# Attention bias of the first head pair in a buffer of its own, one reciprocal write per pair, and token chunks of 512 first queries

## Chip, cores and metric

One Trainium2 chip, one core. The metric is the device time of one execution in microseconds (us). The kernel before took 1145.42 us (median of three runs, 1142.89 to 1146.14).

## What is computed

Attention with a relative-position bias (batch 8, 8 heads, 576 positions, head size 64), and then a gated two-layer network on its 4608 tokens. The sizes below are those of the inputs; everything is float32.

```python
def _attn_ref(q, k, v, w1, b1, w2):
    B, H, S, D = q.shape                        # 8, 8, 576, 64
    scores = (1.0 / np.sqrt(D)) * np.matmul(q, k.transpose(0, 1, 3, 2))
    pos = np.arange(S)
    rel = (pos[:, None] - pos[None, :]).astype(np.float32)
    psi_rel = np.log1p(np.abs(rel))
    psi_i = np.log1p(np.maximum(pos[:, None].astype(np.float32), 1.0))
    x = (psi_rel / psi_i)[..., None]
    h = np.maximum(x @ w1 + b1, 0.0)            # hidden 32
    bias = h @ w2                               # one value per (i, j, head)
    scores = scores + bias.transpose(2, 0, 1)[None, :, :, :]
    scores = scores - np.max(scores, axis=-1, keepdims=True)
    attn = np.exp(scores)
    attn = attn / (np.sum(attn, axis=-1, keepdims=True) + 1e-09)
    return np.matmul(attn, v).astype(np.float32)

def _moe_ref(x, w1, w2, w3, w_out):             # x: 4608 x 512
    a = x @ w1                                  # 512 x 1024
    b = x @ w2
    h = a * b @ w3                              # 1024 x 1024
    return (h @ w_out).astype(np.float32)       # 1024 x 512
```

## The kernel before

It has four stages on one core, and each engine's order within them comes from a table of times that is sorted (`ORDER`, `FIRST`, `AT_...`, one number per step). The table fixes PE (matmuls), ACT (ScalarE), DVE (VectorE) and POOL (GpSimd) up to what the tile scheduler lets float; the order on SP, the queue that issues nearly all DMAs, is the scheduler's own. An engine and a queue run strictly in order: what stands behind a waiting instruction waits too.

**Prologue: the bias.** The bias depends on i, j and the head alone, so it is made once for all batches. There are 36 groups `G` of 16 rows i. For each group DVE or ACT makes the hidden layer in four parts (`hidden`, L507 on DVE into `zdve`, 14 buffers; L505 on ACT into `zact`, 6 buffers), PE multiplies by w2 (L522, `bacc`, four PSUM buffers, one or two per group), ACT copies the result, 16 rows x 8 heads on the 128 partitions, to `bev` (L535), and SP writes it to the DRAM tensor `nb_d` (L537), one row of 591 values per row i and head. A `bev` has four buffers (`ep`), so the copies of a group wait for the write of the group four before. The wide groups come first: 576 columns in group 0, 304 around group 18, 576 again in group 35.

`load_bias` (L237 to L240) reads the bias back from `nb_d` as tiles of 128 rows of one head: tiles 0 to 7 (four blocks of 128 rows, even for the first head of the pair, odd for the second) and tile M, the last 64 rows of both heads. A block needs groups up to 7, 15, 23 or 31; M needs all 36.

**Attention.** 32 units, one for each pair of heads `p` and batch `b`. For each unit SP loads q, k and v (`rq`, `rk`, `rv`; those of the first unit's q and k go through ACT's queue), POOL splits q and k into a high and a low part for exact products (`op_g`, L266 and L267: `kh`, `kl`, `qh`, `ql`), PE makes the scores of nine tiles (`op_S`, L283, two PSUM buffers `s`), DVE adds the bias and takes the maximum (`op_T`, L294, needs `nb`), ACT the exponential (`op_E`, L319), PE transposes (L340 and others), and multiplies by v (`op_W`, L403). On DVE the tiles of a unit run in the order 3, 2, 5, 6, 1, 0, M, 4, 7. The output `x` of a unit is not yet divided by the sums and goes to the DRAM tensor `x_d[p]` with one write (L416). At the end of a pair the 72 sums of its eight batches are inverted, transposed to `rt` (L363), and written to `r_d[p]` with two writes per batch, sixteen in all (L329, L330).

**Folding.** Since nothing nonlinear stands between w3 and w_out, the kernel multiplies them once (`fold`, L608 to L628, `wacc` on PE), beside the last units. At the same time the up-projection weights come in as 64-bit numbers and are narrowed (`narrow`: load `wi` at L129, L134 and L138 on ACT, L144 to L166 on DVE, L171 and L172 on POOL, `wi` has two buffers), then split into `wh` and `wl`. ACT and DVE interleave this with the high and low parts of w3 (`w3h` L619, `w3l` L621) and with the split of the first x chunk.

**Chunks.** The 4608 tokens go through the network in nine chunks of 512, in their order in memory. For each, SP loads x and the reciprocals of four pairs (`load_x`: `xr` L643, `rb` L646, a row of r_d broadcast to 64 partitions), DVE multiplies and splits (`split_x`, L652, L658, with POOL's L656 between), PE does the up (L670) and down (L695) products, and SP writes 4 x 128 rows out (L706). The last chunk's output is split over ACT and DVE (L710 to L713).

Of the kernel before, what the change touches and what calls it, by code (L numbers as in the profile page):

```python
# [65 lines left out]
def relpos_attention_moe(  # L66
# [161 lines left out]
    def load_bias(p, t, first=False):  # L228
# [92 lines left out]
    def op_r(u, n):  # L321
        p, b = units[u]
        if n == "":
            nc.vector.tensor_scalar(sums[p], sums[p], 1e-9, None, op0=ALU.add)
            nc.vector.reciprocal(sums[p], sums[p])
        else:
            for c in range(B):
                rows, x = r_d[p][:, c * S:(c + 1) * S], rts[p][9 * c:9 * c + 9]
                nc.sync.dma_start(rows[:, 0:512].rearrange("h (i j) -> h i j", j=P), x[0:8])  # L329
                nc.sync.dma_start(rows[:, 512:S].rearrange("(o h) j -> o h j", o=1), x[8:9])  # L330
# [83 lines left out]
    def op_x(u, n):  # L414
        p, b = units[u]
        nc.sync.dma_start(x_d[p][:, b * S:(b + 1) * S], st[u]["x"])  # L416
# [32 lines left out]
    with ExitStack() as pro:  # L449
        sb = pro.enter_context(tc.tile_pool(name="pro", bufs=1))  # L450
        zp = pro.enter_context(tc.tile_pool(name="zp", bufs=14))
        ep = pro.enter_context(tc.tile_pool(name="ep", bufs=4))
# [59 lines left out]
        def bias_group(G):  # L512
# [16 lines left out]
            for c, acc in zip((0, 512), accs):  # L529
# [6 lines left out]
            r0 = G * GR * NB_W + 1  # L536
            nc.sync.dma_start(  # L537
                nb_d[:, r0:r0 + GR * (NB_W + 1)].rearrange("h (i w) -> i h w", i=GR)[:, :, 0:L + R + 1], ev,
            )
# [31 lines left out]
    NT = CH // P  # L571
    STEP = 7.8
# [67 lines left out]
    def load_x(c):  # L640
        for cc in range(NC):
            xr = xs.tile([P, CH], F32, name=f"xr{cc}", bufs=1)
            nc.sync.dma_start(xr, x_d[cc][:, c * CH:(c + 1) * CH])  # L643
            rb = xs.tile([P, CH], F32, name=f"rb{cc}", bufs=1)
            for h, rows in enumerate((lo, hi)):
                nc.sync.dma_start(rb[rows], r_d[cc][h:h + 1, c * CH:(c + 1) * CH].broadcast_to([64, CH]))  # L646
# [40 lines left out]
    def down(c, ft):  # L687
# [140 lines left out]
```

## Time and profile before

| | us |
|---|---|
| median of the runs | 1145.42 |
| the profiled execution | 1145.79 |
| its span, first to last instruction | 1144.0 |
| PE busy | 1103.3 |
| DVE busy | 632.2 |
| ACT busy | 564.4 |
| POOL busy | 372.0 |
| granted PE clock, mean | 0.989 |

The page divides the span into 40 slices and gives each engine's busy tenths in each; its fourth part is the chain of work that ended last, its fifth the costliest groups of instructions with the idle time before them and what ended it. Rows of busy time by stretches read: start and end, length, busy time of PE, PE's weight loads, DVE, ACT and POOL with their numbers of instructions, then the granted PE clock, the busy share of the 16 DMA engines, and GB/s. A timeline row has the start, the duration, the engine, the line, the operation, output <- input, shapes, the count of merged instructions, and in brackets the idle time before it with what ended it. SPq and ACTq rows are DMA issues: their time is that of the issue, not of the transfer.

### The profile page before, as it was taken

The page shows a single profiled execution, that of the slowest core. Times are in us where ns is not written, and L with a number is a line of the kernel's source. Part 1 is how long each engine was busy: PE and PEld are TensorE (multiplying, and loading weights), DVE is VectorE, ACT ScalarE, POOL GpSimd, SP SyncE. Part 2 cuts the span into 40 slices and gives each one's busy share as a digit, 9 for nine tenths or more (in the row PEclk, how much of TensorE's full clock was granted, in tenths as well). Part 3 has the DMA queues.
Part 4 walks back from the last instruction along what each step waited for, and adds up shares of the span by engine and source line. Part 5 has one row for each costly group of instructions (what it writes and reads, how often), then busy time and mean ns, then how long its engine had stood idle before and what let it go on. Part 6 is the DMA issues. An engine that isn't in the chain of part 4 may idle for free.

```text
span 1144.0 us, 22667 instructions
## 1 busy us (share of the span) xinstructions
PE 1103.3 (96%) x9092; PEld 865.1 (76%) x9092; DVE 632.2 (55%) x1267; ACT 564.4 (49%) x1119; POOL 372.0 (33%) x286
## 2 busy tenths in 40 slices
PE   7669999999999999997999999999999999999998
PEld 3147777777777777775888888888888888888886
DVE  8748997998799799878992312222131312223112
ACT  6669988998898899853542121121212112121211
POOL 0346775676677577364450000000000000000000
PEclk9889999999999999998999999999999999999999
DMA  7874575557555644226331202021121102110101
GB/s 210 259 216 122 176 223 169 158 153 238 155 177 187 190 148 150 89 83 178 111 129 38 74 9 83 19 74 38 53 59 37 56 19 74 37 37 1 37 1 37
DMA packets 61513, 123.15 MB, mean 108 GB/s; under 512 B 9696, under 2 KB 19296, under 8 KB 61408
## 3 DMA queue, kind: packets, MB, share of 16 engines
q1 hardware_dynamic: 60112, 120.21, 33.7%
q8 instruction: 71, 1.16, 0.4%
q10 hardware_dynamic: 1296, 1.49, 0.4%
q14 instruction: 34, 0.28, 0.1%
HBM read 91.76 MB, written 29.92 MB: 106 GB/s over the span
## 4 chain that ended last, share of the span: by engine, by line
PE 82%; DMA 3%; ACT 2%; DVE 2%; issue 1%; POOL 1%; SPq 1%; ACTq 0%; DVEq 0%; POOLq 0%
PE up L670 32%; PE o L695 16%; PE pst L403 14%; PE s L283 13%; PE pst L340 6%; DMA wi<-in_moe_w_dram 2%; PE wacc L628 1%; POOL w L171 1%; ACT pt L365 1%; DMA rb<-r_d 1%; PE pst L347 1%; PE pst L351 0%; ACT pp L319 0%; SPq L329 0%; DVE w3l L621 0%
## 5 line engine op out<-in xcount | busy, mean ns | idle before, releaser
L294 DVE CUSTOM_DVE_ANT_0 ts<-s,nb 128x576 f32<-128x576 f32 x288 | 210.6, 754 | 56.5 <-PE s L283 31.7
L678 DVE TENSOR_TENSOR g<-up,a 128x512 f32<-128x512 f32 x72 | 49.7, 690 | 332.3 <-PE up L670 332.3
L670 PE MATMUL up<-xl,wh 128*128 128x512 f32 x576 | 225.0, 391 | 0.0
L670 PE MATMUL up<-xh,wl 128*128 128x512 f32 x576 | 224.9, 391 | 0.0
L670 PE MATMUL up<-xh,wh 128*128 128x512 f32 x576 | 224.9, 391 | 0.0
L319 ACT ACTIVATE pp<-ts,mx 128x576 f32<-128x576 f32 x256 | 195.8, 771 | 20.7 <-DVE mx L294 18.9
L695 PE MATMUL o<-w3s,gh 128*128 128x512 f32 x576 | 177.4, 389 | 0.0
L403 PE MATMUL pst<-pt,rv 128*64 128x256 f32 (+1 forms) x1280 | 167.5, 407 | 0.6 <-DVE rt L363 0.4
L656 POOL TENSOR_SCALAR xh<-xr 128x512 fp32r<-128x512 f32 x36 | 24.4, 677 | 441.6 <-DVE xr L652 438.2
L675 ACT COPY a<-up 128x512 f32<-128x512 f32 x72 | 42.2, 585 | 247.3 <-PE up L670 247.3
L365 ACT ACTIVATE pt<-pst 128x1024 f32<-128x1024 f32 x128 | 124.1, 1019 | 23.4 <-PE pst L340 23.4
L403 PEld LDWEIGHTS pst<-pt,rv 128*64 128x64 f32 x1280 | 87.6, 136 | 62.2 <-issue 9.0
L681 ACT ACTIVATE gh<-g 128x512 fp32r<-128x512 f32 x72 | 45.5, 632 | 174.6 <-DVE g L678 174.6
L283 PE MATMUL s<-kh,qh 64*128 64x288 f32 x640 | 118.6, 366 | 10.9 <-DVE mx L294 8.7
L670 PEld LDWEIGHTS up<-xh,wl 128*128 128x128 f32 x576 | 108.1, 188 | 23.5
L670 PEld LDWEIGHTS up<-xl,wh 128*128 128x128 f32 x576 | 108.1, 188 | 23.3
L670 PEld LDWEIGHTS up<-xh,wh 128*128 128x128 f32 x576 | 108.1, 188 | 23.3
L695 PEld LDWEIGHTS o<-w3s,gh 128*128 128x128 f32 x576 | 108.1, 188 | 22.7
L695 PE MATMUL o<-w3s,gl 128*128 128x512 f32 x288 | 112.3, 390 | 0.5 <-DVE gl L684 0.5
L340 PE MATMUL pst<-ident,pp 64*128 64x64 f32 x2304 | 102.1, 223 | 0.7 <-ACT pt L365 0.7
L340 PEld LDWEIGHTS pst<-ident,pp 64*128 64x128 f32 x2304 | 96.9, 139 | 6.5 <-ACT pt L365 5.7
L283 PE MATMUL s<-kh,ql 64*128 64x288 f32 x640 | 96.1, 294 | 2.4 <-POOL ql L267 2.4
(92 smaller groups left out, 1655.1 us busy)
## 6 DMA issues: line engine op xcount, KB each, us to landing
rq<-in_q_dram SPq DMA_DIRECT2D x31, 640.0 KB
wi<-in_moe_w_dram SPq DMA_DIRECT2D x32, 512.0 KB
nb_d<-bev SPq DMA_DIRECT2D x36, 295.5 KB
rv<-in_v_dram SPq DMA_DIRECT2D x32, 320.0 KB
x_d<-x SPq DMA_DIRECT2D x32, 288.0 KB
xr<-x_d SPq DMA_DIRECT2D x36, 256.0 KB
rb<-r_d SPq DMA_DIRECT2D x72, 128.0 KB
rk<-in_k_dram SPq DMA_DIRECT2D x31, 288.0 KB
```

The costliest lines, as they stand in the source:

```text
L283: nc.tensor.matmul(s[:, hf, :HS], Q[x][rows, q0:q0 + P], K[y][rows, h * HS:(h + 1) * HS], start=(m == 0), stop=(m == len(ops) - 1),)
L294: nc.vector.tensor_tensor_reduce(out=halves(ts), in0=d.pop(("s", t))[:, :, :HS], in1=halves(NB[p, t]), op0=ALU.add, op1=ALU.min, scale=-1. ...
L319: nc.scalar.activation(pp, ts, AF.Exp, bias=mx, scale=-1.0, accum_out=sums[p][:, 9 * b + col:9 * b + col + 1])
L340: nc.tensor.transpose(ps[0:n, hf, c0:c0 + 64], x[rows], ident[rows, rows])
L365: nc.scalar.activation(o, x, AF.Copy)
L403: nc.tensor.matmul(o, x[:, c0:c0 + D], m, start=(c == 0), stop=(c == 4 and n_m == len(ms) - 1),)
L656: nc.gpsimd.tensor_scalar(xh, xr, 1.0, 1.0, op0=ALU.mult, op1=ALU.mult)
L670: nc.tensor.matmul(acc, l[:, cc], r, start=(n == 0), stop=(n == 3 * NC - 1))
L675: nc.scalar.copy(a, ps[0])
L678: nc.vector.tensor_tensor(g, ps[1], a, op=ALU.mult)
L681: nc.scalar.activation(gh, g, AF.Copy)
L695: nc.tensor.matmul(d["o", t], l[:, sl], folded[ft][r], start=(ft == 0 and n == 0), stop=(ft == NF - 1 and n == 2),)
```

## The change

Five edits, which hang together.

1. The bias of heads 0 and 1 gets a DRAM tensor of its own, `nb_0`. The host reorders the columns of w2 so that the heads of pair 0 are every fourth partition of `bev`. Each group is now written twice: first the 32 partitions of pair 0 to `nb_0`, and, as a step of its own with its own pace (`PACE_D`), all 128 to `nb_d`. The first pair's tiles are read from `nb_0`. `bev` has 18 buffers.
2. The loads of the first unit's q and k and their splits come earlier in the table (`FIRST`).
3. `r_d[p]` takes the layout of `rt`, 8 batches x 9 rows x 128, so that one write of 72 rows replaces sixteen.
4. `x_d[p]` holds the first 512 queries of the eight batches and then their last 64 queries, in two writes per unit. A chunk is one batch's first 512 queries; the eight times 64 last queries form a chunk, which runs eighth, before batch 7 (`SEQ`). Loads and output rows follow; the outputs of that chunk are eight writes of 64 rows.
5. The pool `sm` is opened ahead of `ppool` and `pt`, so it lies at other addresses.

```diff
-LEAD, PACE_B, BUSY_D, BUSY_A, LAG_B = 48.00, 1.25, 1.95, 4.50, 6.15
-FIRST = {"ldk": -15.0, "ldq": -14.0, "ldv": -4.0, "gk": -9.0, "gq": -5.0}
+LEAD, PACE_B, PACE_D, BUSY_D, BUSY_A, LAG_B = 48.00, 1.25, 2.20, 1.95, 4.50, 6.15
+FIRST = {"ldk": -38.0, "ldq": -36.0, "ldv": -4.0, "gk": -32.0, "gq": -30.0}
...
-    r_d = [dram.tile([2, NTOK], F32, name=f"r_d{p}") for p in range(NPAIR)]
+    r_d = [dram.tile([B, 9, P], F32, name=f"r_d{p}") for p in range(NPAIR)]
...
-            rows = nb_v[2 * p + h, r0:r0 + o.shape[0], :]
+            rows = (nb_v[h * NPAIR + p] if p else nb_v0[h])[r0:r0 + o.shape[0], :]
...
-            for c in range(B):
-                rows, x = r_d[p][:, c * S:(c + 1) * S], rts[p][9 * c:9 * c + 9]
-                nc.sync.dma_start(rows[:, 0:512].rearrange("h (i j) -> h i j", j=P), x[0:8])
-                nc.sync.dma_start(rows[:, 512:S].rearrange("(o h) j -> o h j", o=1), x[8:9])
+            nc.sync.dma_start(r_d[p].rearrange("b n j -> (b n) j"), rts[p])
...
-        nc.sync.dma_start(x_d[p][:, b * S:(b + 1) * S], st[u]["x"])
+        nc.sync.dma_start(x_d[p][:, b * 512:(b + 1) * 512], st[u]["x"][:, 0:512])
+        nc.sync.dma_start(x_d[p][:, B * 512 + b * 64:B * 512 + (b + 1) * 64], st[u]["x"][:, 512:S])
...
-        ep = pro.enter_context(tc.tile_pool(name="ep", bufs=4))
+        ep = pro.enter_context(tc.tile_pool(name="ep", bufs=18))
...
-            r0 = G * GR * NB_W + 1
-            nc.sync.dma_start(
-                nb_d[:, r0:r0 + GR * (NB_W + 1)].rearrange("h (i w) -> i h w", i=GR)[:, :, 0:L + R + 1], ev,
-            )
+            for nb, x in ((nb_0, ev[0:P:NPAIR]), (nb_d, ev)):
+                r0 = G * GR * NB_W + 1
+                nc.sync.dma_start(nb[:, r0:r0 + GR * (NB_W + 1)].rearrange("h (i w) -> i h w", i=GR)[:, :, 0:L + R + 1], x)
+                yield
...
-            put(plan, bias_group(G), *(at + d for d in AT_BIAS))
+            put(plan, bias_group(G), *(at + d for d in AT_BIAS), min(-LEAD + AT_BIAS[-1] + 1.0 + G * PACE_D, -0.3 + 0.005 * G))
...
+    sm = att.enter_context(tc.tile_pool(name="sm", bufs=2))
     ppool = att.enter_context(tc.tile_pool(name="ppool", bufs=1))
     pt = att.enter_context(tc.tile_pool(name="pt", bufs=1))
-    sm = att.enter_context(tc.tile_pool(name="sm", bufs=2))
...
+    SEQ = [*range(B - 1), B, B - 1]
...
-            nc.sync.dma_start(xr, x_d[cc][:, c * CH:(c + 1) * CH])
+            nc.sync.dma_start(xr, x_d[cc][:, k * CH:(k + 1) * CH])
...
-                nc.sync.dma_start(rb[rows], r_d[cc][h:h + 1, c * CH:(c + 1) * CH].broadcast_to([64, CH]))
+                if k < B:
+                    o, r = rb[rows], r_d[cc][k:k + 1, 4 * h:4 * h + 4].rearrange("o i j -> o (i j)").broadcast_to([64, CH])
+                else:
+                    o = rb[rows].rearrange("p (b j) -> p b j", b=B)
+                    r = r_d[cc][:, 8, 64 * h:64 * h + 64].rearrange("b (o j) -> o b j", o=1).broadcast_to([64, B, 64])
+                nc.sync.dma_start(o, r)
...
+                if k == B:
+                    nc.scalar.copy(o, d["o", t])
+                    for e, part in enumerate((lo, hi)):
+                        r0 = (2 * t + e) * S + 512
+                        nc.sync.dma_start(out[r0:r0 + 64, :], o[part])
...
-    w2 = inputs["w2"]
+    w2 = inputs["w2"].reshape(hid, pairs, 2).transpose(0, 2, 1).reshape(hid, heads)
```

Three places show what moves. The first is PE's row in the prologue. Before, the first unit's scores (L283) come behind the bias groups 30 (496 columns) and 31 (512), in the midst of group 32:

```order
L522 MATMUL bacc<-zdve,w2b 32x496 x3
L522 MATMUL bacc<-zact,w2b 32x496
L522 MATMUL bacc<-zdve,w2b 32x512 x6
L283 MATMUL s<-kh,qh 128x288 x2
L283 MATMUL s<-kh,ql 128x288
L522 MATMUL bacc<-zact,w2b 32x512
```

In the changed kernel they (now L286) stand between groups 13 (368 columns) and 14 (352), on the way to the narrow ones:

```order
L523 MATMUL bacc<-zdve,w2b 32x368 x4
L286 MATMUL s<-kh,qh 128x288
L523 MATMUL bacc<-zdve,w2b 32x352 x3
L286 MATMUL s<-kh,qh 128x288
L286 MATMUL s<-kh,ql 128x288 x2
L523 MATMUL bacc<-zact,w2b 32x352
L523 MATMUL bacc<-zdve,w2b 32x336 x4
```

22 of the 36 groups now stand behind the first scores, where 4 did.

The second place is SP at the end of the bias, where the loads of tiles 6 and 7 (128x576, and 128x512 with 128x64) and of M (the rows with 64 partitions) are issued. Before:

```order
L237 DMA nb<-nb_d 128x576
L537 DMA nb_d<-bev 16x8x591 x2
L239 DMA nb<-nb_d 128x512
L240 DMA nb<-nb_d 128x64
L254 DMA rq<-in_q_dram 128x1280
L237 DMA nb<-nb_d 64x576
L239 DMA nb<-nb_d 64x512
L240 DMA nb<-nb_d 64x64
```

In the changed kernel (nb_98 is `nb_0`):

```order
L539 DMA nb_98<-bev 16x2x591
L240 DMA nb<-nb_98 128x576
L242 DMA nb<-nb_98 128x512
L243 DMA nb<-nb_98 128x64
L539 DMA nb_d<-bev 16x8x591 x16
L240 DMA nb<-nb_98 64x576
L242 DMA nb<-nb_98 64x512
L243 DMA nb<-nb_98 64x64
L257 DMA rq<-in_q_dram 128x1280
```

Sixteen whole writes now stand between the loads of tiles 6 and 7 and those of M.

The third is SP at the passage from attention to chunks. Before, the loads of the first chunk (xr and rb, four pairs) come ahead of the fifth and sixth weight load:

```order
L129 DMA wi<-in_moe_w_dram 128x4x256 x2
L643 DMA xr_9401<-x_d_98 128x512
L416 DMA x_d_101<-x 128x576
L646 DMA rb_9403<-r_d_102 64x512 x2
L643 DMA xr_9406<-x_d_99 128x512
L646 DMA rb_9408<-r_d_103 64x512 x2
L643 DMA xr_9411<-x_d_100 128x512
L646 DMA rb_9413<-r_d_104 64x512 x2
L643 DMA xr_9416<-x_d_101 128x512
L646 DMA rb_9418<-r_d_105 64x512 x2
L129 DMA wi<-in_moe_w_dram 128x4x256 x2
```

In the changed kernel:

```order
L416 DMA x_d_102<-x 128x512
L417 DMA x_d_102<-x 128x64
L129 DMA wi<-in_moe_w_dram 128x4x256
L647 DMA xr_9410<-x_d_99 128x512
L655 DMA rb_9412<-r_d_103 64x512 x2
L647 DMA xr_9415<-x_d_100 128x512
L655 DMA rb_9417<-r_d_104 64x512 x2
L647 DMA xr_9420<-x_d_101 128x512
L655 DMA rb_9422<-r_d_105 64x512 x2
L647 DMA xr_9425<-x_d_102 128x512
L655 DMA rb_9427<-r_d_106 64x512 x2
L129 DMA wi<-in_moe_w_dram 128x4x256
```

The fifth weight load moved ahead of the twelve loads of the first chunk, and the sixth stayed behind them.

More of the change, by code (lines that the diff above doesn't have):

```diff
@@ L199, in relpos_attention_moe @@
     nb_d = dram.tile([H, (S + 1) * NB_W], F32, name="nb_d")
-    nb_v = nb_d[:, 0:S * NB_W].rearrange("h (i w) -> h i w", w=NB_W)[:, :, NB_L:NB_L + S]
+    nb_0 = dram.tile([2, (S + 1) * NB_W], F32, name="nb_0")
+    nb_v, nb_v0 = (
+        x[:, 0:S * NB_W].rearrange("h (i w) -> h i w", w=NB_W)[:, :, NB_L:NB_L + S] for x in (nb_d, nb_0)
+    )
     x_d = [dram.tile([P, NTOK], F32, name=f"x_d{p}") for p in range(NPAIR)]
-    r_d = [dram.tile([2, NTOK], F32, name=f"r_d{p}") for p in range(NPAIR)]
+    r_d = [dram.tile([B, 9, P], F32, name=f"r_d{p}") for p in range(NPAIR)]
     att, att_r = ctx.enter_context(ExitStack()), ctx.enter_context(ExitStack())
@@ L571, in relpos_attention_moe @@
     NT = CH // P
+    SEQ = [*range(B - 1), B, B - 1]
+    assert NCH == B + 1 and S - 64 == CH
     STEP = 7.8
@@ L640, in load_x @@
     def load_x(c):
+        k = SEQ[c]
         for cc in range(NC):
             xr = xs.tile([P, CH], F32, name=f"xr{cc}", bufs=1)
-            nc.sync.dma_start(xr, x_d[cc][:, c * CH:(c + 1) * CH])
+            nc.sync.dma_start(xr, x_d[cc][:, k * CH:(k + 1) * CH])
             rb = xs.tile([P, CH], F32, name=f"rb{cc}", bufs=1)
             for h, rows in enumerate((lo, hi)):
-                nc.sync.dma_start(rb[rows], r_d[cc][h:h + 1, c * CH:(c + 1) * CH].broadcast_to([64, CH]))
+                if k < B:
[4 more added lines that the diff above has]
+                nc.sync.dma_start(o, r)
             chunks[c]["x"][cc] = (xr, rb)
@@ L702, in down @@
                 o = op.tile([P, DO], F32, name="osb")
-                rows = out[c * CH + t * P:c * CH + (t + 1) * P, :]
-                if c < NCH - 1:
+                k = SEQ[c]
+                r0 = min(k, B - 1) * S + t * P
+                rows = out[r0:r0 + P, :]
+                if k == B:
[3 more added lines that the diff above has]
+                        nc.sync.dma_start(out[r0:r0 + 64, :], o[part])
+                elif c < NCH - 1:
                     nc.scalar.copy(o, d["o", t])
```

## The prediction

> **What bounds the kernel now.** Three views in this order: the page for the share of each engine, the busy time by stretches to see where TensorE (PE) is not full, and the timelines of those stretches to see what ends each gap.
>
> ```profile
> span 1144.0 us, 22667 instructions
> PE 1103.3 (96%) x9092; PEld 865.1 (76%) x9092; DVE 632.2 (55%) x1267; ACT 564.4 (49%) x1119; POOL 372.0 (33%) x286
> ...
> 50.00:60.00 10.00, 5.05 (x21) 1.47 (x23) 1.09 (x3) 5.00 (x12) 9.17 (x6) 0.54 0.59 166
> ...
> 70.00:80.00 10.00, 4.21 (x62) 3.96 (x62) 2.80 (x8) 4.65 (x12) 1.26 (x1) 0.73 0.70 212
> ...
> 300.00:400.00 100.00, 99.57 (x1459) 78.30 (x1461) 85.69 (x197) 89.22 (x182) 68.08 (x50) 1.00 0.58 180
> ...
> 520.00:550.00 30.00, 23.93 (x89) 18.09 (x88) 24.98 (x33) 10.53 (x19) 14.97 (x12) 0.89 0.50 152
> 550.00:1144.00 594.00, 589.46 (x2587) 485.02 (x2585) 179.87 (x260) 121.32 (x209) 45.37 (x50) 1.00 0.15 48
> ```
>
> The second number of a window is its length, the third PE's busy time. PE is full in the attention (99.57 of 100 us) and in the chunks (589.46 of 594). So a change pays only where PE is not full: the bias prologue with the first unit (about 50 to 85 us) and the passage from attention to chunks (about 510 to 540). The profiled execution took 1145.79 us, 1.8 more than its span and 0.4 more than the median of the runs shown; I forecast from 1145.8.
>
> In the first place VectorE (DVE) tells what the first unit waits for:
>
> ```profile
> 5.95 45.14 DVE L507 TENSOR_SCALAR zdve<-tsh,beta 128x576 f32<-128x576 f32 x126
> ...
> 60.69 0.76 DVE L294 CUSTOM_DVE_ANT_0 ts<-s,nb 128x576 f32<-128x576 f32 x1 [9.61 <-PE s L283]
> ...
> 68.21 0.76 DVE L294 CUSTOM_DVE_ANT_0 ts<-s,nb 128x576 f32<-128x576 f32 x1 [4.18 <-DMA nb<-nb_d]
> ...
> 76.68 0.76 DVE L294 CUSTOM_DVE_ANT_0 ts<-s,nb 128x576 f32<-128x576 f32 x1 [6.10 <-DMA nb<-nb_d]
> ```
>
> DVE makes bias inputs without a gap until 51.1, waits 9.6 us for the first scores, and at last for the bias of tile M, the seventh of the unit, until 76.68. DVE works in order, so the unit's last two tiles and all later units stand behind it. **The gate of the prologue is the moment M's bias lands.**
>
> **The change, part by part. The bias.** 36 quarter writes come on top of the 36 whole ones. The queue rows in the section on the change put M's load behind the last 16 whole writes. So nearly all bias traffic still stands ahead of M. The rate and the sizes:
>
> ```profile
> q1 hardware_dynamic: 8066, 15.88, 76.9%
> ...
> nb_d<-bev SPq DMA_DIRECT2D x36, 295.5 KB
> nb<-nb_d SPq DMA_DIRECT2D x5, 288.0 KB
> ...
> 10.85 11.44 SPq L537 DMA_DIRECT2D nb_d<-bev  x10
> ...
> 72.31 0.60 SPq L240 DMA_DIRECT2D nb<-nb_d  x1
> ...
> 40.00:50.00 10.00, 6.57 (x44) 1.82 (x44) 10.00 (x26) 6.69 (x16) 4.19 (x1) 1.00 0.95 318
> ```
>
> The first row is of 10 to 77 us: 15.88 MB in 76.9% of 67 us is 308 GB/s while the engines are busy (318 GB/s at a share of 0.95 around 45 us). A whole write is 0.303 MB, a quarter 0.076, a tile of bias 0.295. From 10.85 us until M lands the changed queue moves 36 x 0.303 + 36 x 0.076 + 9 x 0.295 + two units' q and k (1.90) = 18.2 MB: 59 us at 308 GB/s, so M lands no earlier than 70, and about 74 with 2 us of slow start and 2 us from transfer to use. That would be 2.7 us better than 76.68.
>
> But the scores move too. PE's rows put the first of them (kh,qh) between bias groups 13 and 14, and they need GpSimd (POOL) to split q and k. What POOL does beside DVE's stream:
>
> ```profile
> 45.81 5.80 POOL L266 TENSOR_SCALAR kh<-rk 128x576 fp32r<-128x576 f32 x1 [44.50 <-DMA rk<-in_k_dram]
> ...
> L266 POOL TENSOR_SCALAR kh<-rk x32: 669/680/5804, 45.8 to 455.4; 128x576 fp32r<-128x576 f32 x32
> L266 POOL TENSOR_SCALAR qh<-rq x32: 1260/1268/1279, 53.1 to 451.1; 128x1280 fp32r<-128x1280 f32 x32
> ...
> L267 POOL TENSOR_TENSOR kl<-rk,kh x32: 1401/1427/1434, 51.7 to 456.1; 128x576 fp32r<-128x576 f32 x32
> L267 POOL TENSOR_TENSOR ql<-rq,qh x32: 2880/2932/2942, 54.4 to 452.5; 128x1280 fp32r<-128x1280 f32 x32
> ...
> 23.63 2.29 PE L522 MATMUL bacc<-zdve,w2b 128*32 128x368 f32 x12
> ...
> 17.54 1.78 ACT L535 ACTIVATE bev<-bacc,post 128x480 f32<-128x480 f32 x4
> ...
> 41.53 0.34 ACTq L254 DMA_DIRECT2D rk<-in_k_dram  x1
> ```
>
> The split that takes 0.68 us (median) took 5.80 beside the stream, and ended 0.5 us after the stream did: it stood still for as long as DVE ran. I read this as POOL being kept out by a DVE that never pauses. In the change k is asked for within the copies of 17.54, near 18 us, and lands near 22 (4.3 us passed from the request at 41.53 to 45.81), beside the same stream; PE reaches its first score behind the 368-wide group (23.63 here), at about 25.4. Then: PE waits; DVE runs on for its 14 buffers, at 45.14/126 = 0.36 us each or somewhat less (these are narrow), to about 29.5; it stops, and POOL does kh, kl, qh and ql in 0.7 + 1.4 + 1.3 + 2.9 = 6.3 us. Both streams go on at about 36, group 14 is copied out by 37.5, and the stream of inputs ends near 57 in place of 51.1.
>
> Queued behind the wait: bias groups 14 to 35 on PE, their copies on ACT, and on SP the next quarter write, with everything behind it. By then SP has sent 14 quarters, 8 whole writes, two tiles of bias and the first q and k, 5.0 MB or 16 us: the DMA engines run dry near 28 and stand until 37.5. What is left to M is 22 x 0.076 + 28 x 0.303 + 7 x 0.295 + 0.95 = 13.2 MB, 42.7 us: 80.2, and 2 more to use: **82, or 5.5 us later than 76.68.** All behind M moves with it: POOL has the second unit's q and k long before, and PE's two score buffers are full at M, now as before. At 252 GB/s, the mean of 15.88 + 0.95 MB over those 67 us, M would be at 92 and at 335 (318/0.95) at 79. I take 308, the rate of this very stretch.
>
> *The lock.* The Trainium skill, "SBUF — State Buffer", section "Who interferes with whom", says that a two-port DVE instruction and a GpSimd instruction exclude each other only for one whole instruction. By that, POOL would wait for one input of some 0.4 us and not for thirteen; the sum would be 74 and not 82. The 5.80 row speaks against it, though it is one case.
>
> **The reciprocals.** Sixteen writes per pair become one, 60 fewer in all. For the last pair SP spent 485.72 to 495.5 on them, and just behind stood what comes now:
>
> ```profile
> 485.72 0.60 SPq L329 DMA_DIRECT2D r_d<-rt  x1
> ...
> 495.56 0.35 SPq L416 DMA_DIRECT2D x_d<-x  x1
> ...
> 493.68 1.66 POOL L171 TENSOR_TENSOR w<-w,wi 128x512 f32<-128x512 f32 x1 [2.53 <-DVE wi L166]
> ...
> 505.02 0.37 SPq L129 DMA_DIRECT2D wi<-in_moe_w_dram  x1
> 509.54 0.34 SPq L643 DMA_DIRECT2D xr<-x_d  x1
> ...
> 515.91 2.29 SPq L646 DMA_DIRECT2D rb<-r_d  x2
> 518.72 2.94 SPq L129 DMA_DIRECT2D wi<-in_moe_w_dram  x2
> ...
> SPq L129 <- POOL w L171: 17.6, 5, 7.2
> ...
> PE pst L335 <- ACT pt L365: 1.1, 3, 0.4
> ```
>
> The weight load behind them waits for POOL to free its buffer (17.6 us over five loads), and POOL freed it at 495.3 (493.68 + 1.66), so the shorter burst gives at most 0.7 us; I take none. At the ends of the other three pairs PE waits 1.1 us in all, and for ACT's copy: nothing. The same holds for 32 more writes of x (0.35 us of SP for the one above), which lie beside the full PE of the attention, and for the chunk of last queries, whose small loads have a whole chunk (594/9 = 66 us) to land in at a DMA share of 0.15; if that cover were gone, PE would wait for them once.
>
> **The passage.** There the order on SP matters: the fifth weight load (wi) now stands ahead of the twelve loads of the first chunk. Its row above was sent at 518.72 and hurt:
>
> ```profile
> 508.60 0.70 ACT L134 ACTIVATE wmag<-wi 128x512 f32<-128x512 f32 x1 [5.56 <-DMA wi<-in_moe_w_dram]
> ...
> 524.20 0.66 ACT L134 ACTIVATE wmag<-wi 128x512 f32<-128x512 f32 x1 [7.03 <-DMA wi<-in_moe_w_dram]
> ...
> 525.99 0.80 PE L628 MATMUL wacc<-woh,w3h 128*128 128x512 f32 x1 [3.85 <-ACT w3h L619]
> ...
> 524.89 0.43 DVE L144 TENSOR_SCALAR wmag<-wmag 128x512 f32<-128x512 f32 x1 [4.46 <-ACT wmag L134]
> ...
> 536.43 0.68 DVE L621 TENSOR_TENSOR w3l<-w3s,w3h 128x512 fp32r<-128x512 f32 x1
> ...
> 511.90 1.67 POOL L171 TENSOR_TENSOR w<-w,wi 128x512 f32<-128x512 f32 x1 [2.36 <-DVE wi L166]
> ```
>
> Its buffer is free at 513.6 (511.90 + 1.67); sent then, with the 3.5 us from the load at 505.02 to its use at 508.60, it is there at 517.1 and not 524.2. PE's wait of 3.85 us goes. Late next is DVE: it takes the first chunk's x in the same order, and those loads start at 514 and not 509.54, and the sixth weight behind them is as late as now. DVE could begin at 520.4 (524.89 - 4.46) and reach the w3l of 536.43 after the same 11.5 us, at 532.0; I add 1.7 for its wait on the sixth weight. PE ends the folding **2.7 us earlier** (bounds: 0, if the x loads come too late, and 5.0, the shares of 3.85 and of the slow clock after it that DVE could give back).
>
> **Sum:** 1145.8 + 5.5 - 2.7 = **1148.6**, a gain in one place eaten by the other.
>
> **The rivals.**
> - *POOL is not kept out.* Then no stall, M at 74: -2.7 - 2.7, 1140.4. For it: one long split only, which could be a first use. Against: it ended with the stream, and a first use of 5.8 us would stall PE as well.
> - *Slower beyond doubt: the queue runs no faster than its mean of 252 GB/s*, since quarter writes cost nearly what whole ones do to issue (a tiny r_d write took 0.60 us of SP). M at 92: +15 - 2.7, 1158. It decides from about 285 GB/s down.
> - *The change does better than the order says*: M's small read overtakes the writes queued ahead of it. The unit then runs on from 57 and M is needed near 67: about -10 - 2.7, 1133. Against: here M's last piece was sent at 72.31 and used 4.4 us later, and 308 GB/s bring 1.3 MB in that time.
>
> **How the numbers follow.** About 0.3% (3.4 us) is what a measurement can tell from no change. The forecast has 0.57, with its own range 1144 to 1154: M between 79 and 85, the passage between 0 and 5. POOL not kept out 0.20, the slow queue 0.12, M overtaking 0.11. Faster than 1142.4 are most of the second (0.15), nearly all of the last (0.10) and little of the first: 0.27. Slower than 1149.2 are under half of the first (0.26) and the slow queue: 0.38. The rest, 0.35, is the same. The range 1138 to 1157 leaves out most of the two far rivals.
>
> **What would show it.** A gap of about 6 us in DVE's L508 stream near 30, with kh, kl, qh, ql back to back inside it; a dry DMA slice behind it; the first ts at 57 to 58; M's ts near 82 with the longest wait of DVE on nb<-nb_0; ACT's wait of 7.03 us at the fifth weight gone, and the folding about 3 us shorter. A stream that ends at 51, or M before 75, would make the prediction wrong.

## The result, and the profile after

The changed kernel took **1160.22 us** (median of four runs, 1159.32 to 1162.27), the kernel before 1145.54 beside it (four runs, 1142.89 to 1146.14): a ratio of 1.0135, 95% interval 1.0115 to 1.0156, so 1.2 to 1.6% **slower**. Forecast were 1148.6 with a range of 1138 to 1157. The profiled execution took 1160.22 us with a span of 1158.4, that of before 1145.79: 14.4 us more.

The page of the changed kernel has the same number of instructions and the same busy time of PE as before. What was added is waiting:

```profile
span 1158.4 us, 22667 instructions
PE 1103.3 (95%) x9092; PEld 864.7 (75%) x9092; DVE 634.5 (55%) x1267; ACT 563.9 (49%) x1119; POOL 375.1 (32%) x286
```

Busy time by stretches of the changed kernel, with the columns of before (start and end, length, PE, weight loads, DVE, ACT, POOL, granted PE clock, share of the DMA engines, GB/s):

```profile
20.00:50.00 30.00, 22.13 (x145) 7.69 (x142) 20.65 (x62) 15.38 (x37) 14.08 (x4) 0.77 0.53 156
...
30.00:40.00 10.00, 8.16 (x34) 2.58 (x38) 3.95 (x10) 3.00 (x7) 4.17 (x3) 0.50 0.30 79
40.00:50.00 10.00, 9.28 (x82) 3.39 (x74) 8.66 (x27) 6.96 (x18) 0.00 (x0) 0.82 0.50 120
50.00:60.00 10.00, 9.35 (x76) 3.03 (x75) 10.00 (x27) 10.00 (x23) 0.00 (x0) 1.00 0.83 248
60.00:70.00 10.00, 2.37 (x41) 0.89 (x40) 1.48 (x4) 4.54 (x13) 2.25 (x2) 0.87 0.91 304
70.00:80.00 10.00, 3.98 (x24) 2.94 (x24) 2.71 (x8) 0.00 (x0) 3.95 (x3) 0.50 0.95 309
80.00:90.00 10.00, 0.00 (x0) 0.00 (x0) 0.00 (x0) 0.52 (x1) 0.40 (x4) 0.50 0.99 314
300.00:400.00 100.00, 99.34 (x1415) 76.91 (x1411) 86.18 (x197) 89.62 (x185) 71.03 (x50) 1.00 0.56 175
```

From 300 to 400 us nothing has changed. From 80 to 90 nearly all stands still (ACT and POOL start again at 89.5) but the DMA engines, which are full. From 20 to 50 it is the other way round: DMA has a share of 0.53, where the same stretch of before had this:

```profile
20.00:50.00 30.00, 24.26 (x181) 8.56 (x176) 30.00 (x89) 21.99 (x51) 4.19 (x1) 1.00 0.92 291
```

So transfers that ran beside the making of the bias now run after it, with nothing beside them. DVE's timeline of the changed kernel shows the same from the side of the waiting engine; the second row from the end is tile 1, the last is M:

```profile
5.35 22.69 DVE L508 TENSOR_SCALAR zdve<-tsh,beta 128x576 f32<-128x576 f32 x63
33.29 1.71 DVE L508 TENSOR_SCALAR zdve<-tsh,beta 128x304 f32<-128x304 f32 x3 [5.25 <-PE bacc L523]
...
44.14 17.07 DVE L508 TENSOR_SCALAR zdve<-tsh,beta 128x368 f32<-128x368 f32 x45 [0.55 <-PE bacc L523]
69.73 0.76 DVE L297 CUSTOM_DVE_ANT_0 ts<-s,nb 128x576 f32<-128x576 f32 x1 [8.52 <-ACT bev L536]
...
90.38 0.76 DVE L297 CUSTOM_DVE_ANT_0 ts<-s,nb 128x576 f32<-128x576 f32 x1 [14.41 <-ACT pp L322]
...
93.15 0.76 DVE L297 CUSTOM_DVE_ANT_0 ts<-s,nb 128x576 f32<-128x576 f32 x1 [1.25 <-ACT pp L322]
```

The stream of inputs ends at 61.2 instead of 51.1, the first scores are taken at 69.73 instead of 60.69, and M is used at 93.15 instead of 76.68: **16.5 us later**. The time behind that moment is 1160.22 - 93.15 = 1067.1 us, and was 1145.79 - 76.68 = 1069.1: 2 us are won back. The loss is all in the prologue.

DVE's 14.41 us end on ACT's exponential. ACT's own timeline and SP's (the queue that issues the DMAs; `nb` is `nb_0` in these names, or a tile of bias) say what ACT waited for:

```profile
68.64 1.06 ACT L536 ACTIVATE bev<-bacc,post 128x16 f32<-128x16 f32 x3 [2.54 <-DMA nb_d<-bev]
89.48 0.78 ACT L322 ACTIVATE pp<-ts,mx 128x576 f32<-128x576 f32 x1 [19.77 <-DMA nb<-nb]
```

```profile
37.19 0.51 SPq L539 DMA_DIRECT2D nb<-bev  x1
...
69.73 0.52 SPq L539 DMA_DIRECT2D nb<-bev  x1
...
71.89 13.97 SPq L539 DMA_DIRECT2D nb_d<-bev  x16
85.91 1.05 SPq L240 DMA_DIRECT2D nb<-nb  x1
```

The last quarter (a write to `nb_0`) is sent at 69.73. Then sixteen whole writes go out, and only then, at 85.91, M's load. The first exponential, whose scores DVE took at 69.73, starts at 89.48. The wait is put down to a load, but that is the transfer that came last of several. Two gates stand at one place here. M's load is queued behind the sixteen writes; and the exponentials' buffers lie where bev lay, so that they wait until the last of these writes has read it. The last copy into bev had itself waited for a whole write (the 2.54 us of its row), since a group takes the buffer of the group eighteen before it. The built programs place the pools thus (bytes within a partition):

```
            before             changed
post        64704 ..  64848    64704 ..  64848   (scale that ACT's bev copies read)
bev        110944 .. 120412   110944 .. 153564
ts         140992 .. 150208    61632 ..  70848
ppM, pp     61632 ..  99520    76672 .. 114560
pt          99520 .. 140992   114560 .. 156032
```

Before, pp shared nothing with bev; with sm ahead it moved up by 15 KB and covers the first two of the now 18 buffers, and ts covers what the last bev copy reads, which is its wait of 8.52. Two buffers are enough to hold up the exponentials until the pool's last write: taken in turn, these two last held groups 18 and 19, whose whole writes were sent at 66.83 and 68.89, ahead of the sixteen, and yet the first exponential starts at 89.48. So the pool seems to be handed on only as a whole; no run tests that by itself. The experiments test this reading against the prediction's: POOL's stall and a steady queue.

### The profile page after: what moved, and what is told of

Its sections match the earlier page's. It is cut to its first block, busy times and chain, and to the rows that moved or that the text cites. A ratio compares the mean times of both kernels' runs of the same rounds, so it can differ in the third digit from the quotient of the medians.

```text
span 1158.4 us, 22667 instructions
## 1 busy us (share of the span) xinstructions
PE 1103.3 (95%) x9092; PEld 864.7 (75%) x9092; DVE 634.5 (55%) x1267; ACT 563.9 (49%) x1119; POOL 375.1 (32%) x286
## 4 chain that ended last, share of the span: by engine, by line
PE 83%; DMA 4%; ACT 4%; DVE 3%; POOL 2%; SPq 2%; issue 2%; ACTq 0%; DVEq 0%; POOLq 0%
PE up L679 31%; PE o L704 16%; PE pst L403 14%; PE s L286 13%; PE pst L340 6%; DMA wi<-in_moe_w_dram 2%; PE bacc L523 1%; SPq L539 1%; POOL w L171 1%; ACT bev L536 1%; POOL kh L269 1%; PE wacc L631 1%; ACT pt L365 1%; DMA nb_d<-bev 1%; PE pst L347 1%
## 5 line engine op out<-in xcount | busy, mean ns | idle before, releaser
L322 ACT ACTIVATE pp<-ts,mx 128x576 f32<-128x576 f32 x256 | 195.8, 771 | 38.3 <-DMA nb<-nb 19.8
L286 PE MATMUL s<-kh,qh 64*128 64x288 f32 x640 | 120.0, 369 | 31.4 <-DVE mx L297 24.4
L286 PEld LDWEIGHTS s<-kh,qh 64*128 64x128 f32 x640 | 64.1, 195 | 54.2 <-DVE mx L297 29.0
```

Source lines behind the costliest of these rows:

```text
L286: nc.tensor.matmul(s[:, hf, :HS], Q[x][rows, q0:q0 + P], K[y][rows, h * HS:(h + 1) * HS], start=(m == 0), stop=(m == len(ops) - 1),)
L322: nc.scalar.activation(pp, ts, AF.Exp, bias=mx, scale=-1.0, accum_out=sums[p][:, 9 * b + col:9 * b + col + 1])
```

## The experiments

**Scores late again.** Edit 2 alone is undone:

```diff
-FIRST = {"ldk": -38.0, "ldq": -36.0, "ldv": -4.0, "gk": -32.0, "gq": -30.0}
+FIRST = {"ldk": -15.0, "ldq": -14.0, "ldv": -4.0, "gk": -9.0, "gq": -5.0}
```

> The changed kernel with the first unit's loads, splits and scores back at their old places (edit 2 undone alone). Theory, stall: in the changed kernel PE stood about 7.5 us near 25 to 33 us for POOL's split, ran at half clock until about 43, and the DMA engines starved meanwhile. Then here the input stream ends near 51 instead of 61, the DMA share of 25 to 50 us is above 0.85 instead of 0.45, M is used near 81 instead of 93.2, and the time is 1145 to 1150 instead of 1160. Rival, buffers: the 18 bev buffers, read by the late whole writes until 89, hold the exponentials up whatever the stall does; then the first exponential still starts near 89 and the time stays at 1157 to 1160.

Measured: 1155.9 us, ratio 1.0092 (1.0070 to 1.0113). Between the theories, and neither is right. The stream of inputs does end at 50.5 and M is used at 88.34, but the split met the late end of the stream:

```profile
40.64 10.43 POOL L269 TENSOR_SCALAR kh<-rk 128x576 fp32r<-128x576 f32 x1 [39.34 <-DMA rk<-in_k_dram]
51.15 1.40 POOL L270 TENSOR_TENSOR kl<-rk,kh 128x576 fp32r<-128x576 f32 x1
```

The row of POOL's timeline shows 10.43 us for an instruction of 0.68, a stall longer than the 8.90 of the changed kernel, at another place. And the last quarter went out at 64.93, the first exponential came at 84.67: 19.7 us between them, where the changed kernel has 89.48 - 69.73 = 19.8.

**Split on DVE.** To take POOL out of the first unit without moving it:

```diff
-        nc.gpsimd.tensor_scalar(h, x, 1.0, 1.0, op0=ALU.mult, op1=ALU.mult)
-        nc.gpsimd.tensor_tensor(l, x, f(h), op=ALU.subtract)
+        e = nc.vector if u == 0 else nc.gpsimd
+        e.tensor_scalar(h, x, 1.0, 1.0, op0=ALU.mult, op1=ALU.mult)
+        e.tensor_tensor(l, x, f(h), op=ALU.subtract)
```

> The changed kernel with the first unit's four split instructions on DVE instead of POOL, at the same early place; the other 31 units as they are. Theory, lock: POOL is kept out by DVE's stream, so taking POOL out of this step ends PE's long wait; DVE pays about 4 us for the four instructions, the stream ends near 55, PE's clock stays up, M is used near 78, and the time is 1144 to 1148. Rival, early scores are bad wherever they are split (k and q arrive too late, or two score buffers block PE): PE still stands over 4 us near 25 and the time stays at 1156 or more.

Measured: 1150.78 us, ratio 1.0046 (1.0032 to 1.0060), 9.4 us better than the changed kernel. PE's long wait is gone and its clock stays up. But M is used at 84.27 and not 78. Its stretches show why:

```profile
20.00:30.00 10.00, 8.82 (x52) 3.25 (x49) 9.93 (x26) 6.62 (x16) 0.00 (x0) 1.00 0.86 290
30.00:40.00 10.00, 10.00 (x81) 4.32 (x81) 10.00 (x33) 8.01 (x20) 0.00 (x0) 1.00 0.66 178
40.00:50.00 10.00, 10.00 (x70) 3.69 (x67) 10.00 (x28) 10.00 (x24) 0.00 (x0) 1.00 0.83 247
...
70.00:80.00 10.00, 0.00 (x0) 0.00 (x0) 0.00 (x0) 0.00 (x0) 0.00 (x0) 0.50 0.98 332
```

With no stall, and PE and DVE busy throughout, the DMA engines still move only 178 GB/s from 30 to 40: the queue has nothing to send, since the table gives a whole write a turn only every 2.20 (`PACE_D`) while a group comes every 1.25. From 70 to 80 the held-back writes run alone. Again 19.8 us pass from the last quarter (60.80) to the first exponential (80.60).

**M ahead of the late writes.** A number in the table lets M's load stand behind three of the sixteen:

```diff
-... + G * PACE_D, -0.3 + 0.005 * G))
+... + G * PACE_D, 4.5 + 0.005 * G))
```

> The changed kernel with the load of tile M behind three of the sixteen late whole writes instead of all sixteen. Theory, two gates: the exponentials' buffers lie where bev lay, and wait for the last of the whole writes, so moving M alone gains nothing: the first exponential starts near 90 and the time is 1158 to 1161. Rival, M's landing alone is the gate, as the prediction had it: M is there at about 79, and the time falls to 1146 to 1149.

Measured: 1161.2 us, ratio 1.0134 (1.0113 to 1.0155): as the changed kernel. M's load went out at 72.32, and ACT's timeline shows the other gate alone, now by its right name:

```profile
89.96 0.78 ACT L322 ACTIVATE pp<-ts,mx 128x576 f32<-128x576 f32 x1 [21.96 <-DMA nb_d<-bev]
```

**Writes not held back.** `PACE_D` is 1.25, so each whole write stands right behind its quarter. It was tried with the early splits on POOL (the changed kernel), with late scores, and with the split on DVE:

```diff
-LEAD, PACE_B, PACE_D, BUSY_D, BUSY_A, LAG_B = 48.00, 1.25, 2.20, 1.95, 4.50, 6.15
+LEAD, PACE_B, PACE_D, BUSY_D, BUSY_A, LAG_B = 48.00, 1.25, 1.25, 1.95, 4.50, 6.15
```

> The changed kernel with the whole writes no longer held back (their pace 1.25 instead of 2.20, so each stands right behind its quarter write); the early splits on POOL stay. Theory, held-back writes: the sixteen whole writes behind the last quarter cost 17 to 20 us of every variant of the changed kernel, the DMA engines having been idle a third of the time before; without them M is used 5 to 8 us after the last quarter write (near 70), at 75 to 78, though POOL is kept out as before: 1142 to 1146. Rival, the prediction's model (the queue is never short of work but for the stall, so only the sum of bytes counts): M at 82 to 93 as before, 1149 to 1160. Rival, stall alone: nothing changes, 1158 to 1161.

> The changed kernel with whole writes not held back and the first unit's loads, splits and scores at their old late places. Theory: the held-back writes were its cost of 17 to 20 us less 7 us of bytes: M used at 73 to 77 instead of 88.3, 1142 to 1146. Rival, POOL's late stall (kh until 51) is the cost: 1150 or more.

> The changed kernel with both mended: whole writes not held back, the first unit's splits on DVE. Theory: the two add up; from 150 us before in the time scale of the earlier run (1150.8) the held-back part of 17 to 20 us less about 7 us of bytes that still have to go: M used near 73, 1138 to 1142, faster than before. Rival: quarter writes on top of all whole ones fill the queue (18.2 MB instead of 15.9), M at 78 or later: 1145 or more.

Measured medians in us, with those from above:

| first scores, and split on | not held back | held back | M used at |
|---|---|---|---|
| late, POOL | 1150.2 | 1155.9 | 82.45, 88.34 |
| early, POOL | 1151.5 | 1160.2 (the change) | 85.36, 93.15 |
| early, DVE | 1147.0 | 1150.8 | 79.25, 84.27 |

Against the kernel before the left column has ratios of 1.0034 (1.0021 to 1.0048), 1.0042 (1.0028 to 1.0057) and 1.0008 (0.9996 to 1.0020). Holding the writes back costs 5.7, 8.7 and 3.8 us. All three came out above what I had expected by 4 us or more, and within the ranges of their rivals: the held-back writes are not the whole cost. The stretches of the last one show the rest:

```profile
30.00:40.00 10.00, 10.00 (x81) 4.26 (x81) 10.00 (x33) 7.93 (x19) 0.00 (x0) 1.00 0.93 291
40.00:50.00 10.00, 10.00 (x67) 3.66 (x64) 10.00 (x28) 10.00 (x24) 0.00 (x0) 1.00 0.90 273
50.00:60.00 10.00, 7.02 (x75) 3.40 (x70) 5.63 (x14) 5.56 (x16) 0.00 (x0) 0.90 0.89 266
60.00:70.00 10.00, 1.09 (x6) 0.74 (x6) 0.77 (x2) 0.00 (x0) 2.65 (x2) 0.50 0.94 308
```

Now the DMA engines are nearly full from 30 to 70, PE and DVE are done with the bias at 55, and the queue itself is the bound, at 266 to 308 GB/s. Into it the change puts 36 x 0.076 = 2.7 MB of quarter writes that the kernel before did not have, 9 us at 300 GB/s. Edits 3 to 5 without edit 1, and with the scores at their late place, took 1143.9 (split on POOL) and 1137.5 us (on DVE) in the runs below, 6.3 and 9.6 less than the first and the last row; the second pair differs in the place of the scores too.

**No whole writes at all**, with the early splits on POOL as in the changed kernel; pairs 1 to 3 then get the bias of pair 0:

```diff
-            rows = (nb_v[h * NPAIR + p] if p else nb_v0[h])[r0:r0 + o.shape[0], :]
+            rows = nb_v0[h][r0:r0 + o.shape[0], :]
...
-            for nb, x in ((nb_0, ev[0:P:NPAIR]), (nb_d, ev)):
+            for nb, x in ((nb_0, ev[0:P:NPAIR]),):
```

> The changed kernel without any of the 36 whole writes; the three other pairs read the bias of the first pair, so the work behind the prologue has the same size (their values are those of other heads). The early splits on POOL stay. Theory, whole writes: they are what stands between the last quarter and the first unit; without them the input stream still ends near 61 (POOL's stall and the half clock stay), the last quarter is sent near 65, M is used near 70 instead of 93: 1136 to 1140. Rival, stall: POOL's stall and the slow PE behind it are most of the 16 us: 1148 or more.

Measured: 1138.82 us, ratio 0.9937 (0.9922 to 0.9952). POOL's stall is there (`kh` takes 8.37 us), PE runs at half clock behind it, and M is used at 72.41. The whole writes, with the room that they keep, are worth 21.4 us of the changed kernel's time. What the stall costs without them no run shows.

**Exponentials apart from bev.** Not held back and split on DVE, with the pools in the old order and 12 bev buffers:

```diff
-        ep = pro.enter_context(tc.tile_pool(name="ep", bufs=18))
+        ep = pro.enter_context(tc.tile_pool(name="ep", bufs=12))
...
-    sm = att.enter_context(tc.tile_pool(name="sm", bufs=2))
     ppool = att.enter_context(tc.tile_pool(name="ppool", bufs=1))
     pt = att.enter_context(tc.tile_pool(name="pt", bufs=1))
+    sm = att.enter_context(tc.tile_pool(name="sm", bufs=2))
```

> The changed kernel with whole writes not held back and the split on DVE (1147.0), and with ppool and pt ahead of sm and 12 bev buffers instead of 18, so that no bev lies under the exponentials' buffers. Theory: the first exponential, at 75.1 before, starts near 58, but tile 6 and M still wait for the queue (the load of M was sent at 73.3): M used 1 to 2 us earlier, 1145 to 1146.5. Rival: the buffers were the gate there: M used near 75, 1142 to 1143.

Measured: 1147.65 us, ratio 1.0016 (1.0006 to 1.0026). The first exponential starts at 61.98 instead of 75.11, and M is used at 78.26 instead of 79.25. That one us is less than the passage lost by the old order of the pools (below). So lifting this gate alone gains nothing either. That left open whether the held-back writes still cost when both gates are lifted:

```diff
+        gap = pro.enter_context(tc.tile_pool(name="gap", bufs=1)).tile([P, 912], F32, name="gap")
         ep = pro.enter_context(tc.tile_pool(name="ep", bufs=18))
...
-... + G * PACE_D, -0.3 + 0.005 * G))
+... + G * PACE_D, 4.5 + 0.005 * G))
```

> The changed kernel with the load of tile M behind three of the sixteen late whole writes, and bev 3.6 KB higher, so that neither ts nor the exponentials' buffers lie on it; only the transposed copies pt still do. Theory, held-back writes: what reads bev late blocks whatever is laid over it. M is used near 80 and the first exponential starts near 70, but the first copy into pt waits for the last whole write, near 89 to 90, and only 4 to 5 us are won: 1154 to 1157. Rival: M and the exponentials were the only gates, and the rest floats: the first copy into pt near 76, 1146 to 1149.

Measured: 1156.54 us, ratio 1.0095 (1.0082 to 1.0109). M is used at 77.58, the first exponential starts at 68.95, and ACT's next row stands at the third gate, the copy into pt, which still lies on bev:

```profile
90.83 1.02 ACT L365 ACTIVATE pt<-pst 128x1024 f32<-128x1024 f32 x1 [14.99 <-DMA nb_d<-bev]
```

The sixteen writes keep 16 of 18 buffers, 38 KB of each partition, the last of them until 90 us, and the attention needs that room from 70 on. 3.7 us are won; the wait has moved and stays.

**Edits 3 to 5 alone**; edits 1 and 2 are taken out of the change:

```diff
-FIRST = {"ldk": -38.0, "ldq": -36.0, "ldv": -4.0, "gk": -32.0, "gq": -30.0}
+FIRST = {"ldk": -15.0, "ldq": -14.0, "ldv": -4.0, "gk": -9.0, "gq": -5.0}
...
-        ep = pro.enter_context(tc.tile_pool(name="ep", bufs=18))
+        ep = pro.enter_context(tc.tile_pool(name="ep", bufs=4))
...
-            for nb, x in ((nb_0, ev[0:P:NPAIR]), (nb_d, ev)):
+            for nb, x in ((nb_d, ev),):
```

> The kernel before with edits 3, 4 and 5 alone: one reciprocal write per pair, x in two parts with chunks of first and of last queries, the pool sm ahead. The bias is as before. Theory: the passage gives about 1.9 us (the folding ends 2.7 earlier, 0.8 given back in the first chunk), but with sm ahead the exponentials' buffers end up on two of the four bev buffers and wait for the last whole write, which costs 0 to 2.5 us near 75: 1143.5 to 1146, within 0.3% of before. Rival: the placement of sm costs nothing: 1143.5 or less. Second rival: the passage's gain was only there because the attention came late: 1145.5 or more with the first exponential no later than before.

Measured: 1143.92 us, ratio 0.9982 (0.9972 to 0.9992): a gain of 2 us whose interval just leaves out no change. The first exponential does wait for the last whole write here (it starts at 70.89, and at 66.98 before), but M is used at 75.59, 1.1 us earlier than before.

**The kernel before, with the split on DVE** (the three lines shown above), and then with edits 3 to 5 added, the same with sm at its old place, and with edit 5 alone:

> The kernel before with the first unit's four split instructions on DVE instead of POOL, at their old late place. Theory, lock: POOL stood 5.8 us beside DVE's stream here too, so the scores no longer block the last bias groups, PE's wait near 50 to 60 goes, the DMA share of 50 to 55 us rises from 0.16 to over 0.8, M is used near 72 instead of 76.7: 1140 to 1143. Rival: DVE's 3.5 us for the split delay the stream by as much and eat it: 1145 to 1147.

> The kernel before with edits 3, 4 and 5 and the first unit's four split instructions on DVE: the bias is written and read as before. Theory: the two gains stand in different stages and add: 2 us of the passage (1143.9 against 1146.0) and 7 us of the prologue (1139.0 against 1146.2), so 1136.5 to 1138. Rival: with sm ahead the exponentials wait for the last whole write, and that takes the place of the wait that DVE's split removed: 1139 or more.

> As the run before it, but the pool sm back behind ppool and pt (edit 5 undone). Theory: the exponentials' buffers no longer lie on bev, the first exponential starts 2 to 4 us earlier, but the bias of M is the later gate: equal to the run before it within 1 us, 1136 to 1138. Rival: the placement is what costs: 2 us or more faster than the run before it.

> The kernel before with edit 5 alone (the pool sm ahead) and the first unit's splits on DVE: reciprocals, x and chunks as before. Theory: of edits 3 to 5 only the place of sm moves the fifth weight load ahead of the first chunk's loads and shortens the passage: folding from its first to its last w3l product takes 63.8 us as with all three edits, not 66.4 to 67.1 as without edit 5, and the time is 1136 to 1138. Rival: the new layout of r_d and x_d is needed as well: 66 us and 1139 to 1140.

| split on DVE, and | us | ratio | M used at | folding, first to last w3l product |
|---|---|---|---|---|
| nothing else | 1138.95 | 0.9942 (0.9919 to 0.9965) | 69.50 | 66.4 |
| edits 3, 4 | 1140.19 | 0.9948 (0.9935 to 0.9961) | 71.02 | 67.1 |
| edit 5 | 1138.16 | 0.9934 (0.9921 to 0.9948) | 70.36 | 63.8 |
| edits 3, 4, 5 | **1137.48** | 0.9923 (0.9911 to 0.9936) | 71.20 | 63.8 |

DVE's timeline of the first of them shows what the split costs there, and the last row that M waits for no bias any more but for PE's scores:

```profile
45.05 0.46 DVE L267 TENSOR_SCALAR kh<-rk 128x576 fp32r<-128x576 f32 x1
45.54 0.76 DVE L268 TENSOR_TENSOR kl<-rk,kh 128x576 fp32r<-128x576 f32 x1
...
49.93 0.82 DVE L267 TENSOR_SCALAR qh<-rq 128x1280 fp32r<-128x1280 f32 x1
50.78 1.49 DVE L268 TENSOR_TENSOR ql<-rq,qh 128x1280 fp32r<-128x1280 f32 x1
...
69.50 0.76 DVE L295 CUSTOM_DVE_ANT_0 ts<-s,nb 128x576 f32<-128x576 f32 x1 [0.66 <-PE s L284]
```

3.5 us of DVE take the place of a wait of 9.6, and M comes 7.2 us earlier. That the split on POOL is what holds PE up is borne out on the kernel before too, and the version with edits 3 to 5 beats both kernels: 1137.5 us against 1145.9 of before beside it. Edits 3 and 4 change nothing that these runs can tell (+1.2 and -0.7 us). The run with edits 3 and 4 came out 2 us above what I expected: I had not yet seen that the shorter passage hangs on edit 5.

## Why the prediction was wrong

**POOL kept out: right.** POOL's timeline of the changed kernel, and PE's:

```profile
19.67 8.90 POOL L269 TENSOR_SCALAR kh<-rk 128x576 fp32r<-128x576 f32 x1 [18.36 <-DMA rk<-in_k_dram]
28.66 1.40 POOL L270 TENSOR_TENSOR kl<-rk,kh 128x576 fp32r<-128x576 f32 x1
30.02 1.26 POOL L269 TENSOR_SCALAR qh<-rq 128x1280 fp32r<-128x1280 f32 x1
31.36 2.89 POOL L270 TENSOR_TENSOR ql<-rq,qh 128x1280 fp32r<-128x1280 f32 x1
```

```profile
31.33 0.61 PE L286 MATMUL s<-kh,qh 64*128 64x288 f32 x1 [6.64 <-POOL qh L269]
```

The four splits stand back to back behind the end of the stream (5.35 + 22.69 = 28.04) and are done 6.2 us later (6.3 were forecast), PE waits 6.64 us, and the next quarter is sent at 37.19 (37.5). The rival that POOL is not kept out falls. By the rule of the Trainium skill ("SBUF — State Buffer", "Who interferes with whom"), a lock for one whole instruction, POOL would have begun after one input of 0.4 us; the 8.90 row and eight like it (last section) speak against that.

**The step that failed** is the one that follows, "What is left to M is ... 13.2 MB, 42.7 us": the bytes divided by 308 GB/s. That is the rate while the DMA engines are busy (15.88 MB in 76.9% of 67 us), so the division takes a queue that always has something to send, but for the stall. It had not. From 40 to 60 us the engines moved 120 and 248 GB/s (rows above), 3.7 MB where 308 GB/s would have been 6.2, a shortfall worth 8 us. From 60 to 90 they moved 304 to 314, as the sum has it. I had counted where M's load stands, and seen the sixteen whole writes ahead of it, but not asked when a write *may* be sent. The table held whole writes back to one per 2.20, and had 4.8 MB left at the end, where nothing else could run: 16 x 0.303 MB at 309 GB/s are 15.7 us.

Late groups behind the stall keep the queue short of work too, and the runs part the two. These are the stretches from 20 to 50 us with the writes held back but no stall (split on DVE), with the stall but the writes not held back, and with neither:

```profile
20.00:50.00 30.00, 28.82 (x196) 11.26 (x197) 29.93 (x85) 24.63 (x58) 0.00 (x0) 1.00 0.78 238
```

```profile
20.00:50.00 30.00, 22.14 (x145) 7.78 (x142) 20.72 (x62) 15.39 (x37) 12.73 (x4) 0.77 0.77 237
```

```profile
20.00:50.00 30.00, 28.82 (x195) 11.24 (x194) 29.93 (x85) 24.72 (x58) 0.00 (x0) 1.00 0.92 292
```

With both the share is 0.53, and before it was 0.92. M is used at 84.27, 85.36 and 79.25 us, and at 93.15 with both. In the prediction's terms: it had M at 74 without the stall and at 82 with it. The stall is sized about right, 8 us for 93.15 - 84.27 = 8.9. The miss was there without it: 84.27 is 10.3 above 74. Of these the held-back writes, which the sum put at nothing, are 84.27 - 79.25 = 5.0 (beside the stall 93.15 - 85.36 = 7.8, and 8.7 in the time). The other 5.3 go with the rate: with neither, the queue moved 273 GB/s from 10 to 78 us, its engines busy for 0.88 of the time, and not 308. These are single executions, and the one with the stall alone took 2.3 us more than the median of its kernel, so the parts are good to some 2 us. What makes the pauses of that last queue no run tells.

**A wait not named.** That 18 buffers instead of 4, and sm ahead, lay bev under the exponentials, and the scale of the last bev copy under ts, was in edits 1 and 5 and not in the prediction: the first ts were forecast for 57 to 58 and came at 69.73. Alone it costs nothing that shows (1143.92 with edit 5, 1147.65 with the pools apart); beside held-back writes it makes a second gate, so that no better place for M's load can help.

**The slow queue** (252 GB/s, 1158 us) came nearest in number, and that is luck: the changed kernel's queue moved 304 to 314 GB/s from 60 to 90, and before that was short of work. In one point the rival was nearer than the forecast: where quarter and whole writes alternate from the start and nothing stalls, the 273 GB/s lie below the 285 at which it was to decide. That a quarter costs nearly what a whole write does to issue is so (0.52 and 0.58 us of SP); whether that makes the pauses is open. And M overtook nothing: its load was sent at 85.91, behind the sixteen writes, and used at 93.15.

**The passage: right in its mechanism, and 2.7 us in the folding.** These are ACT's rows for the fourth to sixth weight loads of the changed kernel, and the folding's w3l products in both kernels (a view by source line: number of instructions, shortest, median and longest duration, first and last start):

```profile
524.82 0.70 ACT L134 ACTIVATE wmag<-wi 128x512 f32<-128x512 f32 x1 [5.52 <-DMA wi<-in_moe_w_dram]
...
534.51 0.67 ACT L134 ACTIVATE wmag<-wi 128x512 f32<-128x512 f32 x1 [1.11 <-DVE wl L594]
...
543.98 0.67 ACT L134 ACTIVATE wmag<-wi 128x512 f32<-128x512 f32 x1 [3.88 <-DMA wi<-in_moe_w_dram]
```

```profile
L631 PE MATMUL wacc<-woh,w3l x64: 388/393/504, 498.2 to 561.9; 128*128 128x512 f32 x64
```

```profile
L628 PE MATMUL wacc<-woh,w3l x64: 388/393/632, 481.9 to 548.3; 128*128 128x512 f32 x64
```

The fifth load's wait of 7.03 is 1.11 now and no longer for a DMA, and the folding takes 63.7 us instead of 66.4. The edit behind it is the fifth alone, which the prediction did not say: in all twelve kernels with it the folding takes 63.7 to 64.0 us, and in the four without it 66.4 to 67.3. In the time the pairs give 0.8 (1138.2 against 1139.0), 2.1 (1143.9 against 1146.0, where M too is used 1.1 us earlier) and 2.7 us (1137.5 against 1140.2); the first of these is within the noise.

**Nothing from the reciprocals, x and the chunk of last queries: right**, to within the 1.2 us of the table above.

**The sum.** Forecast +5.5 - 2.7; measured +16.5 (M) and -2.0 (all behind it), 14.4 in all. What the prologue costs reaches the time one for one: in the eleven kernels with edit 5 in which M's use is the gate (all but the one with both gates lifted), M is used at 70.4 to 93.6 us, and the profiled executions end 1065.6 to 1068.6 us behind it.

## What to carry to other kernels

Sum of bytes over rate gives when a queue is done only if it always has something it may send: look for what holds each transfer back (a pace, a group not yet made, a place in order), and what is left when the makers are done. A transfer that was put off also keeps its source buffer, and whatever is laid over that pool waits; moving the wanted load ahead then gains nothing until all such gates are lifted, and three stood in a row here. And before a step is moved to an earlier place, ask which engine does it there: four small instructions on the engine that was busy anyway were worth 7 us, since the idle engine beside it could not start.

## What the runs showed of the hardware

*How long POOL is kept out.* In all nine kernels in which POOL splits the first k beside DVE's stream, the instruction of 0.68 us ended 0.52 to 0.54 us after the stream did, however early it had begun: it took from 4.62 (edits 3 to 5 alone) over 5.80 (before) and 8.90 (the change) to 10.71 us (late scores, not held back). At 0.36 us for one DVE instruction, it got in between none of some 11 to 28 of them. It is no cost of POOL's first use: in the seven kernels with the split on DVE, POOL's first split took its usual time (`qh` 1.26 us) or 0.67 to 1.27 us (`kh`).

*DVE can be the one that waits.* In the four of those seven without edits 1 and 2, POOL's first `kh` came with the last four inputs of the stream. Here are POOL's rows and those four inputs in the kernel before with the split on DVE:

```profile
51.53 1.27 POOL L267 TENSOR_SCALAR kh<-rk 128x576 fp32r<-128x576 f32 x1 [50.23 <-DMA rk<-in_k_dram]
52.89 1.50 POOL L268 TENSOR_TENSOR kl<-rk,kh 128x576 fp32r<-128x576 f32 x1
```

```profile
L508 DVE TENSOR_SCALAR zdve<-tsh,beta x4: 505/716/1660, 52.2 to 55.0; 128x576 f32<-128x576 f32 x4
```

POOL waited for little more than the DVE instruction in progress, a TENSOR_TENSOR that ended at 52.27, and then DVE's inputs took up to 1.66 us, where one of that width takes 0.51 alone. So POOL is not shut out beside every stream; what lets it in here and not in the nine, no run tells.

*How long the half clock lasts.* PE had stood for 6.64 us until 31.33. The rows of the changed kernel show it busy for 8.16 of the 10 us from 30 to 40 at a clock of 0.50, and for 9.28 of the ten after those at 0.82, which is 3.6 us more at 0.50: some 12 us in all, at work. The Trainium skill ("TensorE: Matmul & The Clock Gate", "What's actually happening") has half clock after an idle window, which agrees, and full clock after about 3.4 us of sustained work, which it does not agree with. Whether narrow matmuls (32 columns of the array) or the short gaps between them are the reason, no run here tells.
